# Three queries before a gate and five after, rows of w_o dealt by hand, and loops on VectorE and ScalarE

## The chip, the core and the metric

The kernel runs on one core of a Trainium2 chip. The metric is the time of one execution on the device in microseconds (us); where several executions are given, their median counts. A profiled execution also has a span, from its first to its last instruction, and all times inside the text are counted from the span's start.

A core has compute engines with a queue of instructions each: TensorE (PE in the profile; its weight loads are PEld), VectorE (DVE), ScalarE (ACT), GpSimd (POOL) and SyncE (SP), which here only issues transfers. Transfers between HBM and the on-chip memory SBUF are carried out by 16 DMA engines, and TensorE writes its sums to PSUM, here eight banks of 512 columns. Engines order themselves by semaphores: an instruction can add to one when it ends, and another can wait until one has reached a value.

## The reference, cut to what matters

One token is decoded: attention of 32 heads over a cache of 8192 keys and values each, with a gate from a small GLU beside it.

```python
xn = _layernorm(x, axis=-1)                      # x: 1 x 1 x 512
q = (xn @ wq).reshape(B, Sq, H, Dh)              # H = 32, Dh = 128
scores = einsum("bhqd,bhkd->bhqk", q, k_cache) * (Dh ** -0.5)
p = softmax(scores)
o = einsum("bhqk,bhkd->bhqd", p, v_cache)        # caches: 1 x 32 x 8192 x 128
s = o.reshape(B, Sq, H * Dh) @ wo                # wo: 4096 x 512
h = sigmoid(xn @ w_gate) * (xn @ w_up)           # 512 x 1376 each
g = silu(h @ w_down)                             # 1376 x 512
return x + s * g
```

All tensors are float32. The two caches are 134 MB each, out of 294 MB that the kernel reads.

## The kernel before

Two heads form a pair; there are 16 pairs (`NP`). A pair's keys are one load of 128 partitions by 16,384 columns (64 KB in each partition, 8.39 MB): 64 partitions for each head, 128 keys of 128 numbers in each. A pair's values have the same form. SBUF holds three slots of this size. K of even pairs goes into slot B, K of odd pairs into A, and V always into C; the last V goes into B, and w_o into C behind it. Before the pairs, A holds the three gate weights and C holds `wq`.

**One pair.** VectorE (`scores`, L295) multiplies the keys by the pair's query and sums over each key's 128 numbers, in two halves (L307, L309), then takes the largest score (L312). TensorE turns that column into a row (L339), VectorE reduces it (L314), TensorE spreads the result (L341), and ScalarE (`softmax`, L317) scales it, takes the exponentials (L323) and keeps their sums. TensorE then multiplies 32 times by V into the PSUM bank `po` (L350), ScalarE copies `po` out (L327), TensorE turns the parts together (L355), and ScalarE stores them in `heads` (L329). TensorE's work on the first 15 pairs is one loop (L385); on VectorE and ScalarE all 16 pairs are written out.

**The order of the loads** is that of SyncE's queue, and no planner changes it: `wq`, the gate, up and down weights, K0 in two halves, then K1 (L360), which waits for the gate because it overwrites the gate's weights, then V0 (L373), which waits for all eight queries because it overwrites `wq`. After that V and K alternate: V of pair n waits until TensorE has done with V of pair n-1 (`s_po`), and K of pair n+2 waits until VectorE has done with K of pair n (`k_free`, L375). K15 and V15 come in two halves. Last comes w_o (L382) in five pieces of 16, 8, 5, 2 and 1 rows in each partition (`WO`), a row having 2 KB, each piece with a semaphore of its own.

**The start.** `queries` (L234) makes the queries on TensorE, four heads at a time, eight times, into PSUM banks 0 to 7 by their number (L237); ScalarE copies each out in two halves (L245). The first four stand before the gate, the other four behind it (L250, L285). Between them VectorE weights the gate's and then the up matrix (`weighted`, L222 and L225), TensorE sums each over the partitions, column by column (L258, L259, into banks 4 and 5), ScalarE takes the sigmoid (L263), VectorE forms `hid` (L266) and weights the down matrix (L269 to L272), and TensorE sums it into `g_ps` (L279), bank 3. ScalarE takes its sigmoid into `g_row` (L283), and VectorE multiplies `g_row` by `g_ps` (L367) after the scores of pair 0. `busy` (L332) runs idle multiplications into `g_ps` near the end.

**The end.** When all heads are there, VectorE divides by the sums and turns the result (L395 to L404, `o_all`), and TensorE multiplies it by w_o, piece by piece as each lands: 24 rows into one bank (L414), which ScalarE copies (L423), then the rest and the copy into another (L418, L427). VectorE multiplies by `g_row` and adds x (L431, L433), and SyncE stores the 2 KB of output (L435).

Of the kernel before, what the change touches and what calls it, by code (L numbers as in the profile page):

```python
# [25 lines left out]
def kernel(  # L26
# [60 lines left out]
    mx = put("mx", 8)  # L87
# [13 lines left out]
    xnb = o1.rearrange("p (k m) -> p k m", m=P)  # L101
# [4 lines left out]
    wq_t = C.rearrange("p (k c) -> p k c", k=KT)  # L106
    wo_t = C.rearrange("p (r e) -> p r e", e=D)

    psum = nc.alloc_psum_tensor("psum", [P, 8 * QT], F32).ap()
    bank = [psum[:, i * QT:(i + 1) * QT] for i in range(8)]  # L110
    po, pt, pm, g_ps, acc, fold_ps, o_ps, oTl = bank


    sems = []
# [1 line left out]
    def semaphore(name):  # L116
        sems.append(nc.alloc_semaphore(name))
        return sems[-1]

    names = "x xr wg wu wd wr wq ka k0 k1 kb va vb".split()  # L120
    d = {n: Count(semaphore(f"d_{n}")) for n in names}
    WO = ((0, 16), (16, 24), (24, 29), (29, 31), (31, 32))
    d_wo = [Count(semaphore(f"d_wo{i}")) for i in range(len(WO))]
    d_v = semaphore("d_v")
# [11 lines left out]
    k_src = k_cache[0].rearrange("h (p j) e -> (h p) (j e)", p=HALF)  # L136
    v_src = v_cache[0].rearrange("h (p j) e -> (h p) (j e)", p=HALF)
    k_slot = lambda n: (B, A)[n % 2]
    k_sem = lambda n: d[f"k{n % 2}"]
    k_free = {}  # L140

    def rows_of(src, n):
        return src[n * P:(n + 1) * P, :]


    xv = x.rearrange("a b d -> (a b d)")
# [5 lines left out]
    d["wg"].by(sp.dma_start(wg_t, w_gate.rearrange("(p k) f -> p k f", k=KT)), 16)  # L152
    d["wu"].by(sp.dma_start(wu_t, w_up.rearrange("(p k) f -> p k f", k=KT)), 16)
    d["wd"].by(sp.dma_start(wd_t, w_down[:FP * P, :].rearrange("(p r) e -> p r e", r=FP)), 16)
    for name, c in (("ka", slice(0, SLOT // 2)), ("k0", slice(SLOT // 2, SLOT))):
        d[name].by(sp.dma_start(B[:, c], rows_of(k_src, 0)[:, c]), 16)


    s_pool.by(pool.memset(ident, 0.0))
# [14 lines left out]
    d["wr"].by(act.dma_start(wd_rest[:FL, :], w_down[FP * P:, :]), 16)  # L174
    dve.memset(st[:, 6:7], EPS)
    dve.memset(rs2, 0.0)
    for b in (4, 5):
        dve.memset(bank[b][:, :FP + 1], 0.0)
    dve.wait_ge(s_pool.sem, 2)
    for g in range(NG):  # L180
# [3 lines left out]
    def self_wait():  # L184
        dve.wait_ge(s_dve.sem, s_dve.n)
# [42 lines left out]
    n_xnb = s_dve.by(dve.tensor_copy(xnb, xn.rearrange("p (k o) -> p k o", o=1).to_broadcast([P, KT, P])))  # L228


    nq = H // NG
    n_qc = []

    def queries(lo, hi):  # L234
        with nc.Fori(lo, hi, engines=[pe.engine]) as t:
            for k in range(KT):
                m = pe.matmul(psum[:, bass.ds(t * QT, QT)], xnb[:, k, :], wq_t[:, k, bass.ds(t * QT, QT)],  # L237
                              start=(k == 0), stop=(k == KT - 1))
            m.then_inc(s_q, 1)
        for t in range(lo, hi):  # L240
            act.wait_ge(s_q, t + 1)
            pairs = slice(t * NG // 2, (t + 1) * NG // 2)
            for a in range(2):
                r = slice(a * HALF, (a + 1) * HALF)
                c = act.copy(q_all[r, pairs, :], bank[t][r, :].rearrange("p (n a d) -> p n a d", a=2, d=Dh)[:, :, a, :])  # L245
            n_qc.append(s_act.by(c))

    pe.wait_ge(d["wq"].sem, 16)
    pe.wait_ge(s_dve.sem, n_xnb)
    queries(0, nq // 2)  # L250

    turned = [bank[nq // 2 + a][:, :FP + 1] for a in range(2)]
    for a, (name, t) in enumerate((("wg", wg_t), ("wu", wu_t))):
        dve.wait_ge(d[name].sem, 16)
        weighted(t[:, 0, :], lambda k: t[:, k, :], lambda k: xn[:, k:k + 1], KT)
# [17 lines left out]
                                             op0=ALU.mult, op1=ALU.add))  # L273
    pool.wait_ge(s_dve.sem, n_wr)
    n_prz = s_pool.by(pool.memset(prz.rearrange("p j a -> p (j a)"), 0.0))
    pe.wait_ge(s_act.sem, n_qc[-1])
    pe.wait_ge(s_dve.sem, n_wr)
    for g in range(NG):
        m = pe.matmul(g_ps[g * GP:g * GP + 1, :GC], ones[:, 0:1], wd_t[:, 0, g * GC:(g + 1) * GC],  # L279
# [2 lines left out]
    act.wait_ge(s_pe.sem, n_gate)  # L282
    n_gs = s_act.by(act.activation(g_row, g_ps[:, :GC], AF.Sigmoid))  # L283
    act.wait_ge(s_pool.sem, n_prz)
    queries(nq // 2, nq)  # L285


    def load_k(n, parts=1):
        w = SLOT // parts
        for i in range(parts):  # L290
            c = k_sem(n) if i == parts - 1 else d["kb"]
            c.by(sp.dma_start(k_slot(n)[:, i * w:(i + 1) * w], rows_of(k_src, n)[:, i * w:(i + 1) * w]), 16)


    def scores(n):  # L295
        kt = k_slot(n).rearrange("p (j d) -> p j d", d=Dh)
        s = sc[n % 2]
        h = NB // 2
        q = q_all[:, n:n + 1, :].to_broadcast([P, h, Dh])
        first = {0: d["ka"], NP - 1: d["kb"]}.get(n)  # L300
        if first:
            dve.wait_ge(first.sem, 16)
        for i in range(2):
            if i == bool(first):
                dve.wait_ge(k_sem(n).sem, 16 * (n // 2 + 1))
            part = kt[:, i * h:(i + 1) * h, :]
            s_dve.by(dve.tensor_mul(part, part, q))  # L307
            self_wait()
            s_dve.by(dve.reduce_sum(s[:, i * h:(i + 1) * h], part, axis=AX.X))  # L309
        k_free[n] = s_dve.n  # L310
        self_wait()
        dve.reduce_max(mx[:, 0:1], s, axis=AX.X).then_inc(s_rm, 1)  # L312
        dve.wait_ge(s_pt, n + 1)
        dve.reduce_max(mx[:1, 2:4], pt[:1, :P].rearrange("p (a m) -> p a m", a=2), axis=AX.X).then_inc(s_am, 1)  # L314


    def softmax(n):  # L317
        act.wait_ge(s_pm, n + 1)
        s_act.by(act.mul(mx[:, 4:6], pm[:, 0:2], -SCALE))  # L319
        act.wait_ge(s_act.sem, s_act.n)  # L320
        for a in range(2):
            r = slice(a * HALF, (a + 1) * HALF)
            e = act.activation(prz[r, :, a], sc[n % 2][r, :], AF.Exp, bias=mx[r, 4 + a:5 + a], scale=SCALE,  # L323
                               accum_out=rs2[r, a:a + 1])
        e.then_inc(s_pr, 1)
        act.wait_ge(s_po, n + 1)
        act.copy(o1, po).then_inc(s_o1, 1)  # L327
        act.wait_ge(s_ot, n + 1)
        s_act.by(act.copy(heads[:, n, :], oTl[:, 0:4]))  # L329


    def busy(count):  # L332
# [37 lines left out]
    for n in range(NP - 1):  # L370
        if n:
            sp.wait_ge(s_po, n)
        sp.dma_start(C, rows_of(v_src, n)).then_inc(d_v, 16)  # L373
# [33 lines left out]
    pe.wait_ge(s_dve.sem, n)  # L407
    FOLD = WO[1][1]
    for (r0, r1), c in zip(WO, d_wo):
        pe.wait_ge(c.sem, 16)  # L410
        for r in range(r0, r1):
            if r < FOLD:
                g = r % NG
                m = pe.matmul(fold_ps[g * GP:g * GP + 1, :], o_all[:, r:r + 1], wo_t[:, r, :],  # L414
                              start=(r < NG), stop=(r >= FOLD - NG))
            else:
                for g in range(NG):
                    m = pe.matmul(acc[g * GP:g * GP + 1, :GC], o_all[:, r:r + 1],  # L418
                                  wo_t[:, r, g * GC:(g + 1) * GC], start=(r == FOLD), stop=(r == RW - 1))
# [49 lines left out]
```

## Time and profile before

| | |
|---|---|
| three runs | 687.00, 687.47 and 690.81 us; median 687.47 |
| the profiled execution | 687.28 us, of which the span has 685.4 |
| read from HBM | 293.67 MB |
| busy in the span | VectorE 588.5 us, TensorE 245.0 (weight loads 92.5), ScalarE 41.5, GpSimd 1.7 |

The page of the profile gives busy time by engine, then the span in 40 slices (a digit is the busy share in tenths; PEclk is the clock granted to TensorE), the DMA queues, the chain of work that ended last, and groups of equal instructions with their line, their number, busy time and mean, and the idle time before them with what ended it. In windows, the columns after the engines' busy time are the granted clock, the DMA share (1.00 is all 16 engines) and GB/s; a transfer's bytes and time count whole in the window where it starts, so that a short window can exceed 1. In the timeline a row is start, duration, engine, line, operation, and the number of instructions merged.

### The profile page before, as it was taken

Reading aid. Unit: us, or ns where it says so; the run is one execution under the profiler, and the core shown is the slowest. Engines: PE = TensorE matmul, PEld = TensorE weight load, DVE = VectorE, ACT = ScalarE, POOL = GpSimd, SP = SyncE. Lnnn points to the kernel's source line nnn. Section 1 sums busy time; section 2 is a strip of 40 time slices with the busy share of each in tenths; the row PEclk is TensorE's granted clock in tenths of the full one; section 3 lists DMA queues with packets and bytes.
Section 4 is the critical chain, followed back from the end, with each engine's and each line's share of the span. In section 5 each row is a group of like instructions: output and inputs, shape, how many; then the busy total and the mean of one; then the engine's idle time right before and its main releaser. Section 6 shows DMA issues by size and latency. Waiting matters only on the chain. (4 is left out here: it accounts for less than half of the span.)

```text
span 685.4 us, 3572 instructions
## 1 busy us (share of the span) xinstructions
PE 245.0 (36%) x1502; PEld 92.5 (14%) x1502; DVE 588.5 (86%) x145; ACT 41.5 (6%) x135; POOL 1.7 (0%) x10
## 2 busy tenths in 40 slices
PE   1595315050412405050422406060422406050486
PEld 0272101010110101010110101010110101010132
DVE  2259999999999999898989899898989899899930
ACT  0010110000000000000010100000010100000010
POOL 0000000000000000000000000000000000000000
PEclk9976856575665657575565757565665756565699
DMA  8999999999999999999999999999999999999996
GB/s 370 419 439 429 437 451 440 432 432 432 433 428 432 428 428 444 444 436 436 432 436 428 432 428 428 436 448 440 428 440 432 432 428 432 428 423 449 425 433 292
DMA packets 6501, 293.74 MB, mean 429 GB/s; under 512 B 760, under 2 KB 768, under 8 KB 1120
## 3 DMA queue, kind: packets, MB, share of 16 engines
q1 hardware_dynamic: 6344, 293.48, 99.1%
q10 hardware_dynamic: 152, 0.20, 0.1%
q8 instruction: 3, 0.05, 0.0%
q14 instruction: 2, 0.02, 0.0%
HBM read 293.67 MB, written 0.00 MB: 428 GB/s over the span
## 5 line engine op out<-in xcount | busy, mean ns | idle before, releaser
L307 DVE TENSOR_TENSOR slot<-slot,q_all 128x8192 f32<-128x8192 f32 x32 | 277.8, 8682 | 21.6 <-DMA slot<-in_A_k_cache_dram 21.6
L309 DVE TENSOR_REDUCE sc<-slot 128x64 f32<-128x8192 f32 x32 | 278.0, 8686 | 1.1
L350 PE MATMUL psum<-slot,prz 128*8 128x512 f32 x1024 | 143.9, 725 | 241.6 <-PEq L134 241.6
L350 PEld LDWEIGHTS psum<-slot,prz 128*8 128x8 f32 x1024 | 29.9, 102 | 342.0 <-issue 341.4
L339 PE MATMUL psum<-ident,mx 128*1 128x128 f32 x32 | 9.2, 387 | 119.4 <-PEq L134 119.4
L237 PE MATMUL psum<-slot,o 128*128 x64 | 32.1, 666 | 9.8 <-DMA slot<-in_A_wq_dram 9.8
L327 ACT COPY o<-psum 128x512 f32<-128x512 f32 x16 | 9.4, 586 | 397.6 <-PE psum L350 397.6
L355 PE MATMUL psum<-pick,o 128*128 128x2 f32 x128 | 16.4, 250 | 12.8 <-PEq L134 12.8
L355 PEld LDWEIGHTS psum<-pick,o 128*128 128x128 f32 x128 | 15.5, 191 | 27.2 <-issue 27.2
L339 PEld LDWEIGHTS psum<-ident,mx 128*1 128x1 f32 x32 | 1.8, 80 | 121.8 <-issue 121.8
L237 PEld LDWEIGHTS psum<-slot,o 128*128 128x128 f32 x64 | 13.6, 217 | 27.1 <-issue 27.1
L344 PE MATMUL psum<-rs,ones 128*128 128x2 f32 x32 | 8.7, 342 | 22.3 <-PEq L134 22.3
L222 DVE TENSOR_SCALAR slot<-slot,xn 128x1376 f32<-128x1376 f32 x2 | 1.9, 936 | 15.5 <-DMA slot<-in_B_w_gate_dram 15.0
L314 DVE TENSOR_REDUCE mx<-psum 1x2 f32<-1x128 f32 x16 | 4.4, 278 | 12.1 <-PE psum L339 12.1
L323 ACT ACTIVATE prz<-sc,mx 64x128 f32<-64x128 f32 x32 | 13.0, 406 | 0.7
L431 DVE TENSOR_TENSOR sc<-g_row,psum 128x128 f32<-128x128 f32 x1 | 0.3, 290 | 13.1 <-PE psum L418 13.1
L319 ACT ACTIVATE mx<-psum 128x2 f32<-128x2 f32 x16 | 2.8, 173 | 143.2 <-PE psum L341 143.2
L341 PE MATMUL psum<-mx,ones 1*128 1x2 f32 x32 | 8.6, 336 | 7.4 <-PEq L134 7.4
L344 PEld LDWEIGHTS psum<-rs,ones 128*128 128x128 f32 x32 | 7.8, 305 | 23.9 <-issue 23.9
L225 DVE SCALAR_TENSOR_TENSOR slot<-slot,xn 128x1376 f32<-128x1376 f32 x6 | 9.9, 1652 | 0.2
L395 DVE RECIPROCAL heads<-heads 128x32 f32<-128x32 f32 x1 | 0.4, 355 | 11.1 <-ACT heads L329 11.1
L341 PEld LDWEIGHTS psum<-mx,ones 1*128 1x128 f32 x32 | 7.7, 297 | 14.7 <-issue 14.7
(67 smaller groups left out, 84.0 us busy)
## 6 DMA issues: line engine op xcount, KB each, us to landing
slot<-in_A_k_cache_dram SPq DMA_DIRECT2D x4, 4096.0 KB, 45.5
slot<-in_A_v_cache_dram SPq DMA_DIRECT2D x2, 4096.0 KB, 37.5
slot<-in_A_wo_dram SPq DMA_DIRECT2D x1, 4096.0 KB, 20.7
slot<-in_B_w_gate_dram SPq DMA_DIRECT2D x1, 2752.0 KB, 28.2
slot<-in_B_w_up_dram SPq DMA_DIRECT2D x1, 2752.0 KB, 34.3
slot<-in_B_w_down_dram SPq DMA_DIRECT2D x1, 2560.0 KB, 39.8
slot<-in_A_wo_dram SPq DMA_DIRECT2D x1, 2048.0 KB, 25.2
slot<-in_A_wo_dram SPq DMA_DIRECT2D x1, 1280.0 KB, 27.7
```

The lines of the kernel that those rows point to most:

```text
L225: s_dve.by(dve.scalar_tensor_tensor(acc, t(k), col(k), acc, op0=ALU.mult, op1=ALU.add))
L237: m = pe.matmul(psum[:, bass.ds(t * QT, QT)], xnb[:, k, :], wq_t[:, k, bass.ds(t * QT, QT)], start=(k == 0), stop=(k == KT - 1))
L307: s_dve.by(dve.tensor_mul(part, part, q))
L309: s_dve.by(dve.reduce_sum(s[:, i * h:(i + 1) * h], part, axis=AX.X))
L314: dve.reduce_max(mx[:1, 2:4], pt[:1, :P].rearrange("p (a m) -> p a m", a=2), axis=AX.X).then_inc(s_am, 1)
L323: e = act.activation(prz[r, :, a], sc[n % 2][r, :], AF.Exp, bias=mx[r, 4 + a:5 + a], scale=SCALE, accum_out=rs2[r, a:a + 1])
L327: act.copy(o1, po).then_inc(s_o1, 1)
L339: pe.matmul(pt[:1, :P], mx[:, 0:1], ident, start=True, stop=True).then_inc(s_pt, 1)
L341: pe.matmul(pm[:, 0:2], ones[:1, :], mx[:1, 2:4], start=True, stop=True).then_inc(s_pm, 1)
L344: pe.matmul(oTl[:, 2:4], ones, rs2, start=True, stop=True)
L350: m = pe.matmul(po[g * GP:g * GP + 2 * ROWS, :], prz[:, j * ROWS:(j + 1) * ROWS, :], v[:, j * QT:(j + 1) * QT], start=(j < NG), stop=(j >= ...
L355: m = pe.matmul(oTl[:, 0:2], o1[:, b * Dh:(b + 1) * Dh], pick[:, 2 * b:2 * b + 2], start=(b == 0), stop=(b == ROWS - 1))
```

## The change

- **Queries.** Three stand before the gate instead of four, and five behind it. The first three use banks 0 to 2; the five use banks 1 to 5. The columns of gate and up move from banks 4 and 5 to 6 and 7, and `g_ps` becomes `po` (bank 0), while `busy` writes to bank 3, now called `idle`. TensorE's wait for ScalarE's copies ahead of the gate goes. Because `po` is overwritten by pair 0, VectorE multiplies `g_row` before the scores of pair 0.
- **Loops.** VectorE runs `scores` in a loop over two pairs, eight times; ScalarE runs `softmax` for pair 0, a loop over two pairs seven times, and pair 15 apart. The query's place in `q_all` and the place in `heads` come from a register. Semaphores that were counted up (`s_dve`, `k_free`, `s_pt`, `s_pm`, `s_po`, `s_ot`) are now waited for and taken down again by the waiting engine, in an instruction of its own (`take`), and `s_kf` and `s_vf` tell SyncE how many K and V slots have come free; `s_vf` is raised by ScalarE instead of TensorE. Each half of K has a semaphore; where K comes whole, SyncE raises the second itself after issuing the load.
- **w_o.** Of the first piece's 16 rows in each partition, 12 are loaded as before. The last four (8 KB in each partition) are loaded for partitions 0 to 79 in one transfer, and for partitions 80 to 127 in four transfers of 12 partitions. All six raise the first piece's semaphore.

```diff
-    po, pt, pm, g_ps, acc, fold_ps, o_ps, oTl = bank
+    po, pt, pm, idle, acc, fold_ps, o_ps, oTl = bank
+    g_ps = po
...
+    def load_k(n, parts=1):
+        w = SLOT // parts
+        for i in range(parts):
+            d[f"{'kh'[i]}{n % 2}"].by(sp.dma_start(k_slot(n)[:, i * w:(i + 1) * w], rows_of(k_src, n)[:, i * w:(i + 1) * w]), 16)
+        if parts == 1:
+            sp.sem_inc(d[f"h{n % 2}"].sem, 16)
...
-    for b in (4, 5):
+    for b in (6, 7):
         dve.memset(bank[b][:, :FP + 1], 0.0)
...
-    nq = H // NG
+    nq, n0 = H // NG, 3
...
-    queries(0, nq // 2)
-
-    turned = [bank[nq // 2 + a][:, :FP + 1] for a in range(2)]
+    queries(0, n0, 0)
+
+    turned = [bank[6 + a][:, :FP + 1] for a in range(2)]
...
-    pe.wait_ge(s_act.sem, n_qc[-1])
     pe.wait_ge(s_dve.sem, n_wr)
...
-    queries(nq // 2, nq)
+    queries(n0, nq, 1)
...
+    def tell_and_take(engine, sem, other):
+        engine.wait_ge(sem, 1).then_inc(other, 1)
+        take(engine, sem)
...
+        q = q_all[:, bass.ds(n, 1), :].to_broadcast([P, h, Dh])
         for i in range(2):
-            if i == bool(first):
-                dve.wait_ge(k_sem(n).sem, 16 * (n // 2 + 1))
+            take(dve, d[f"{'kh'[i]}{odd}"].sem, 16)
             part = kt[:, i * h:(i + 1) * h, :]
-            s_dve.by(dve.tensor_mul(part, part, q))
-            self_wait()
-            s_dve.by(dve.reduce_sum(s[:, i * h:(i + 1) * h], part, axis=AX.X))
-        k_free[n] = s_dve.n
-        self_wait()
+            dve.tensor_mul(part, part, q).then_inc(s_own, 1)
+            take(dve, s_own, i + 1)
+            dve.reduce_sum(s[:, i * h:(i + 1) * h], part, axis=AX.X).then_inc(s_own, 1)
+        tell_and_take(dve, s_own, s_kf)
         dve.reduce_max(mx[:, 0:1], s, axis=AX.X).then_inc(s_rm, 1)
-        dve.wait_ge(s_pt, n + 1)
+        take(dve, s_pt)
...
-        act.wait_ge(s_po, n + 1)
+        tell_and_take(act, s_po, s_vf)
         act.copy(o1, po).then_inc(s_o1, 1)
...
-    for n in range(NP):
-        if n % (NG // 2) == 0:
-            dve.wait_ge(s_act.sem, n_qc[n // (NG // 2)])
-        scores(n)
-        if n == 0:
-            dve.wait_ge(s_act.sem, n_gs)
-            s_dve.by(dve.tensor_mul(g_row, g_row, g_ps[:, :GC]))
-        softmax(n)
+    dve.wait_ge(s_act.sem, n_gs)
+    s_dve.by(dve.tensor_mul(g_row, g_row, g_ps[:, :GC]))
+    with nc.Fori(0, NP // 2, engines=[dve.engine]) as t:
+        for a in range(2):
+            dve.wait_ge(s_act.sem, n_qc[-a])
+            scores(t * 2 + a, a)
+    softmax(0, 0)
+    with nc.Fori(0, NP // 2 - 1, engines=[act.engine]) as t:
+        for a in range(2):
+            softmax(t * 2 + a + 1, 1 - a)
+    s_act.by(softmax(NP - 1, 1))
...
-            sp.wait_ge(s_po, n)
+            sp.wait_ge(s_vf, n)
...
-            sp.wait_ge(s_dve.sem, k_free[n])
+            sp.wait_ge(s_kf, n + 1)
...
     for (r0, r1), c in zip(WO, d_wo):
-        c.by(sp.dma_start(wo_t[:, r0:r1, :], wo.rearrange("(p r) e -> p r e", r=RW)[:, r0:r1, :]), 16)
+        few = FEW if r0 == 0 else 0
+        load_wo(c, r0, r1 - few)
+        if few:
+            load_wo(c, r1 - few, r1, 0, P - 4 * 12)
+            for p in range(P - 4 * 12, P, 12):
+                load_wo(c, r1 - few, r1, p, p + 12)
```

On VectorE, where the gate ends and the pairs begin, there stood (`slot_56` is B, `slot_55` is A, `sc_61` and `sc_62` are the two score tiles; x3 and the like are equal instructions in a row):

```order
L272 SCALAR_TENSOR_TENSOR slot_55<-wd_rest,hid,slot_55 96x512
L307 TENSOR_TENSOR slot_56<-slot_56,q_all 128x8192
L309 TENSOR_REDUCE sc_61<-slot_56 128x64
L307 TENSOR_TENSOR slot_56<-slot_56,q_all 128x8192
L309 TENSOR_REDUCE sc_61<-slot_56 128x64
L312 TENSOR_REDUCE mx<-sc_61 128x1
L314 TENSOR_REDUCE mx<-psum 1x2
L367 TENSOR_TENSOR g_row<-g_row,psum 128x128
```

and there stands now, with the line numbers of the changed kernel (`ISA` computes the query's place):

```order
L280 SCALAR_TENSOR_TENSOR slot_55<-wd_rest,hid,slot_55 96x512
L362 TENSOR_TENSOR g_row<-g_row,psum 128x128
L363 UNCONDITIONAL_BRANCH
L308 ISA
L308 TENSOR_TENSOR slot_56<-slot_56,q_all 128x8192
L310 TENSOR_REDUCE sc_61<-slot_56 128x64
L308 TENSOR_TENSOR slot_56<-slot_56,q_all 128x8192
L310 TENSOR_REDUCE sc_61<-slot_56 128x64
L312 TENSOR_REDUCE mx<-sc_61 128x1
L314 TENSOR_REDUCE mx<-psum 1x2
```

The multiplication of `g_row` has moved from behind the scores of pair 0 to ahead of them, and the scores stand in a loop; the semaphore instructions of `take` are not among these rows.

On SyncE, the end of the queue of loads was (`slot_57` is C):

```order
L379 DMA slot_56<-in_A_v_cache_dram 128x8192 x2
L382 DMA slot_57<-in_A_wo_dram 128x8192
L382 DMA slot_57<-in_A_wo_dram 128x4096
L382 DMA slot_57<-in_A_wo_dram 128x2560
L382 DMA slot_57<-in_A_wo_dram 128x1024
L382 DMA slot_57<-in_A_wo_dram 128x512
```

and is now:

```order
L382 DMA slot_56<-in_A_v_cache_dram 128x8192 x2
L387 DMA slot_57<-in_A_wo_dram 128x6144
L387 DMA slot_57<-in_A_wo_dram 80x2048
L387 DMA slot_57<-in_A_wo_dram 12x2048 x4
L387 DMA slot_57<-in_A_wo_dram 128x4096
L387 DMA slot_57<-in_A_wo_dram 128x2560
L387 DMA slot_57<-in_A_wo_dram 128x1024
L387 DMA slot_57<-in_A_wo_dram 128x512
```

The first piece of w_o has become six loads; the other four stand as before.

On ScalarE, the copies of the queries stand on both sides of the gate's two sigmoids, two to a query. Before:

```order
L245 COPY q_all<-psum 64x256 x8
L263 ACT_TABLE_LOAD
L263 ACTIVATE sg<-psum 128x11
L283 ACTIVATE g_row<-psum 128x128
L245 COPY q_all<-psum 64x256 x8
```

and now:

```order
L253 COPY q_all<-psum 64x256 x6
L271 ACT_TABLE_LOAD
L271 ACTIVATE sg<-psum 128x11
L290 ACTIVATE g_row<-psum 128x128
L253 COPY q_all<-psum 64x256 x10
```

Two copies, those of one query, have moved behind the gate, as that query's multiplications have on TensorE.

More of the change, by code (lines that the diff above doesn't have):

```diff
@@ L118, in semaphore @@
         return sems[-1]
-    names = "x xr wg wu wd wr wq ka k0 k1 kb va vb".split()
+    names = "x xr wg wu wd wr wq k0 k1 h0 h1 va vb".split()
     d = {n: Count(semaphore(f"d_{n}")) for n in names}
+    FEW = 4
     WO = ((0, 16), (16, 24), (24, 29), (29, 31), (31, 32))
@@ L128 @@
     s_pt, s_pm, s_po, s_ot = (semaphore(n) for n in ("s_pt", "s_pm", "s_po", "s_ot"))
+    s_own, s_kf, s_aown, s_vf = (semaphore(n) for n in ("s_own", "s_kf", "s_aown", "s_vf"))
     held = list(sems)
@@ L138 @@
     k_slot = lambda n: (B, A)[n % 2]
-    k_sem = lambda n: d[f"k{n % 2}"]
-    k_free = {}
     def rows_of(src, n):
         return src[n * P:(n + 1) * P, :]
+    def load_k(n, parts=1):
[4 more added lines that the diff above has]
+            sp.sem_inc(d[f"h{n % 2}"].sem, 16)
     xv = x.rearrange("a b d -> (a b d)")
@@ L154 @@
     d["wd"].by(sp.dma_start(wd_t, w_down[:FP * P, :].rearrange("(p r) e -> p r e", r=FP)), 16)
-    for name, c in (("ka", slice(0, SLOT // 2)), ("k0", slice(SLOT // 2, SLOT))):
-        d[name].by(sp.dma_start(B[:, c], rows_of(k_src, 0)[:, c]), 16)
+    load_k(0, 2)
     s_pool.by(pool.memset(ident, 0.0))
@@ L228, with queries @@
     n_xnb = s_dve.by(dve.tensor_copy(xnb, xn.rearrange("p (k o) -> p k o", o=1).to_broadcast([P, KT, P])))
-    nq = H // NG
+    nq, n0 = H // NG, 3
     n_qc = []
-    def queries(lo, hi):
+    def queries(lo, hi, first):
         with nc.Fori(lo, hi, engines=[pe.engine]) as t:
             for k in range(KT):
-                m = pe.matmul(psum[:, bass.ds(t * QT, QT)], xnb[:, k, :], wq_t[:, k, bass.ds(t * QT, QT)],
-                              start=(k == 0), stop=(k == KT - 1))
+                m = pe.matmul(psum[:, bass.ds(t * QT - (lo - first) * QT, QT)], xnb[:, k, :],
+                              wq_t[:, k, bass.ds(t * QT, QT)], start=(k == 0), stop=(k == KT - 1))
             m.then_inc(s_q, 1)
@@ L244, in queries @@
                 r = slice(a * HALF, (a + 1) * HALF)
-                c = act.copy(q_all[r, pairs, :], bank[t][r, :].rearrange("p (n a d) -> p n a d", a=2, d=Dh)[:, :, a, :])
+                c = act.copy(q_all[r, pairs, :], bank[first + t - lo][r, :].rearrange("p (n a d) -> p n a d", a=2, d=Dh)[:, :, a, :])
             n_qc.append(s_act.by(c))
@@ L284 @@
     act.wait_ge(s_pool.sem, n_prz)
-    queries(nq // 2, nq)
[L288 to L297, printed above, removed]
+    queries(n0, nq, 1)
+    def tell_and_take(engine, sem, other):
+        engine.wait_ge(sem, 1).then_inc(other, 1)
+        take(engine, sem)
@@ L298, in scores @@
+    def scores(n, odd):
+        kt = k_slot(odd).rearrange("p (j d) -> p j d", d=Dh)
+        s = sc[odd]
         h = NB // 2
[L299 to L302, printed above, removed]
+        q = q_all[:, bass.ds(n, 1), :].to_broadcast([P, h, Dh])
         for i in range(2):
-            if i == bool(first):
-                dve.wait_ge(k_sem(n).sem, 16 * (n // 2 + 1))
+            take(dve, d[f"{'kh'[i]}{odd}"].sem, 16)
@@ L314, in scores, with softmax @@
         dve.reduce_max(mx[:1, 2:4], pt[:1, :P].rearrange("p (a m) -> p a m", a=2), axis=AX.X).then_inc(s_am, 1)
[L317 to L320, printed above, removed]
+    def softmax(n, odd):
+        take(act, s_pm)
+        act.mul(mx[:, 4:6], pm[:, 0:2], -SCALE).then_inc(s_aown, 1)
+        take(act, s_aown)
         for a in range(2):
             r = slice(a * HALF, (a + 1) * HALF)
-            e = act.activation(prz[r, :, a], sc[n % 2][r, :], AF.Exp, bias=mx[r, 4 + a:5 + a], scale=SCALE,
+            e = act.activation(prz[r, :, a], sc[odd][r, :], AF.Exp, bias=mx[r, 4 + a:5 + a], scale=SCALE,
@@ L324, in softmax @@
                                accum_out=rs2[r, a:a + 1])
         e.then_inc(s_pr, 1)
-        act.wait_ge(s_po, n + 1)
+        tell_and_take(act, s_po, s_vf)
         act.copy(o1, po).then_inc(s_o1, 1)
-        act.wait_ge(s_ot, n + 1)
-        s_act.by(act.copy(heads[:, n, :], oTl[:, 0:4]))
+        take(act, s_ot)
+        return act.copy(heads[:, bass.ds(n, 1), :], oTl[:, 0:4].rearrange("p (o c) -> p o c", o=1))
     def busy(count):
         for _ in range(count):
-            pe.matmul(g_ps, ones, q_all[:, :QT // Dh, :], start=True, stop=True)
+            pe.matmul(idle, ones, q_all[:, :QT // Dh, :], start=True, stop=True)
@@ L371, with load_wo @@
         if n:
-            sp.wait_ge(s_po, n)
+            sp.wait_ge(s_vf, n)
         sp.dma_start(C, rows_of(v_src, n)).then_inc(d_v, 16)
         if n + 2 < NP:
-            sp.wait_ge(s_dve.sem, k_free[n])
+            sp.wait_ge(s_kf, n + 1)
             load_k(n + 2, 2 if n + 2 == NP - 1 else 1)
-    sp.wait_ge(s_dve.sem, k_free[NP - 2])
+    sp.wait_ge(s_kf, NP - 1)
     for name, c in (("va", slice(0, SLOT // 2)), ("vb", slice(SLOT // 2, SLOT))):
         d[name].by(sp.dma_start(B[:, c], rows_of(v_src, NP - 1)[:, c]), 16)
-    sp.wait_ge(s_po, NP - 1)
+    sp.wait_ge(s_vf, NP - 1)
+    wo_src = wo.rearrange("(p r) e -> p r e", r=RW)
+    def load_wo(c, r0, r1, p0=0, p1=P):
+        c.by(sp.dma_start(wo_t[p0:p1, r0:r1, :], wo_src[p0:p1, r0:r1, :]), 16)
     for (r0, r1), c in zip(WO, d_wo):
-        c.by(sp.dma_start(wo_t[:, r0:r1, :], wo.rearrange("(p r) e -> p r e", r=RW)[:, r0:r1, :]), 16)
+        few = FEW if r0 == 0 else 0
[4 more added lines that the diff above has]
+                load_wo(c, r1 - few, r1, p, p + 12)
     pe.wait_ge(s_act.sem, n_qc[-1])
@@ L409 @@
     for (r0, r1), c in zip(WO, d_wo):
-        pe.wait_ge(c.sem, 16)
+        pe.wait_ge(c.sem, c.n)
         for r in range(r0, r1):
```

## The prediction

> **What bounds the kernel now.** I read the page first: the total, the DMA slices and the queues.
>
> ```profile
> span 685.4 us, 3572 instructions
> DMA  8999999999999999999999999999999999999996
> DMA packets 6501, 293.74 MB, mean 429 GB/s; under 512 B 760, under 2 KB 768, under 8 KB 1120
> q1 hardware_dynamic: 6344, 293.48, 99.1%
> q8 instruction: 3, 0.05, 0.0%
> q14 instruction: 2, 0.02, 0.0%
> ```
>
> All but the first and the last slice show 9, and q1, on which SyncE's loads run, fills 99.1% of what 16 DMA engines could do in the whole span. So the kernel is 293.74 MB through 16 busy DMA engines: 429 / 16 = 26.8 GB/s for each, or 0.306 us for 8 KB. A compute engine matters only where it lets a DMA engine run dry, or behind the last landing. The groups of instructions and the DMA issues say how far VectorE is from doing that.
>
> ```profile
> L307 DVE TENSOR_TENSOR slot<-slot,q_all 128x8192 f32<-128x8192 f32 x32 | 277.8, 8682 | 21.6 <-DMA slot<-in_A_k_cache_dram 21.6
> L414 PE MATMUL psum<-slot,o_all 128*1 128x512 f32 x48 | 7.0, 748 | 2.3 <-DMA slot<-in_A_wo_dram 2.3
> DMA to landing us min/median/max: 27.1/29.3/30.0
> slot<-in_A_k_cache_dram SPq DMA_DIRECT2D x14, 41.8
> ```
>
> VectorE waits for K 21.6 us in nine waits, 2.4 us each: it is quicker than the DMA. A load of 8.39 MB takes 8.39 / 0.429 = 19.6 us; V (the third row) lands 27.1 to 30.0 us after its issue and K after 41.8, so each load stands in the queue for 7.5 us or more before its turn. That is the cover for whatever delays an issue.
>
> The last landings are read from windows of half a microsecond and from the chain that ended last.
>
> ```profile
> 679.50:680.00 0.50, 0.41 (x4) 0.00 (x0) 0.00 (x0) 0.02 (x1) 0.00 (x0) 1.00 0.97 385
> 680.00:680.50 0.50, 0.00 (x0) 0.00 (x0) 0.00 (x0) 0.50 (x1) 0.00 (x0) 1.00 0.53 205
> 680.50:681.00 0.50, 0.32 (x12) 0.31 (x16) 0.00 (x0) 0.06 (x1) 0.00 (x0) 1.00 0.31 123
> 681.00:681.50 0.50, 0.50 (x28) 0.47 (x21) 0.00 (x0) 0.00 (x0) 0.00 (x0) 1.00 0.16 61
> 681.50:682.00 0.50, 0.50 (x29) 0.47 (x22) 0.00 (x0) 0.00 (x0) 0.00 (x0) 1.00 0.25 70
> 682.00:682.50 0.50, 0.50 (x25) 0.31 (x14) 0.00 (x0) 0.00 (x0) 0.00 (x0) 1.00 0.01 4
> q8 instruction: 1, 0.02, 4.8%
> ```
>
> The last two columns are the DMA share and GB/s. Until 680.0 all engines run; then 0.53, 0.31, 0.16 of them, and after 682.0 one row of 2 KB (4 GB/s for 0.5 us) is left. The 0.25 holds a fetch of code that comes after the loads (last row, of the window 681.5 to 683.1: 4.8% of 16 x 1.6 us = 1.23 us on one engine); without it about 0.1. So the engines end over 2 us, two or three of them late. Evened out they would end at 680.0 + 0.5 x (0.53 + 0.31 + 0.16 + 0.25 + 0.01) - 1.23 / 16 = 680.55, against about 682.15. **The most that evenness can bring is 1.6 us**, and nothing in this change cuts bytes.
>
> ```profile
> 2.00:2.50 0.50, 0.00 (x0) 0.00 (x0) 0.00 (x0) 0.00 (x0) 0.09 (x1) 1.00 4.70 1573
> 2.50:3.50 1.00, 0.00 (x0) 0.00 (x0) 0.71 (x8) 0.00 (x0) 0.70 (x4) 1.00 0.66 262
> 1.02 0.39 SPq L148 DMA_DIRECT2D slot<-in_A_wq_dram  x1
> ```
>
> The first load's rows are 65,536 bytes and count whole where they start: 1573 x 0.5 = 786 KB, 12 engines, start by 2.5, and 262 KB, four engines, only up to 1 us later. After that all run without a pause, so who starts late should end late.
>
> **Three and five queries.** The timeline around the gate:
>
> ```profile
> 38.08 5.03 DVE L225 SCALAR_TENSOR_TENSOR slot<-slot,xn 128x1376 f32<-128x1376 f32 x3
> 40.32 4.47 PE L258 MATMUL psum<-ones,slot 128*128 128x1 f32 x20
> 44.97 4.65 PE L258 MATMUL psum<-ones,slot 128*128 128x1 f32 x20
> 58.53 8.68 DVE L307 TENSOR_TENSOR slot<-slot,q_all 128x8192 f32<-128x8192 f32 x1
> 58.75 0.61 PE L279 MATMUL psum<-slot,ones 128*1 128x128 f32 x8 [8.81 <-DVE slot L272]
> 59.42 0.33 SPq L292 DMA_DIRECT2D slot<-in_A_k_cache_dram  x1
> 59.42 0.28 ACT L283 ACTIVATE g_row<-psum 128x128 f32<-128x128 f32 x1 [14.10 <-PE psum L279]
> 68.28 0.75 ACT L245 COPY q_all<-psum 64x256 f32<-64x256 f32 x2 [2.69 <-PE psum L237]
> 71.72 0.75 ACT L245 COPY q_all<-psum 64x256 f32<-64x256 f32 x2 [2.69 <-PE psum L237]
> 75.14 0.33 SPq L373 DMA_DIRECT2D slot<-in_A_v_cache_dram  x1
> ```
>
> A query costs TensorE 71.72 - 68.28 = 3.44 us. With one less, the gate columns start near 36.9 instead of 40.32; the up columns must then wait for VectorE (38.08 + 5.03 = 43.11) and start at 43.2 instead of 44.97. So `hid`, the gate and the issue of K1 come 1.75 us earlier: K1 at 57.7.
>
> ```profile
> 58.00:60.00 2.00, 1.25 (x9) 0.64 (x10) 2.00 (x2) 0.28 (x1) 0.31 (x1) 0.50 1.06 459
> 60.00:62.00 2.00, 2.00 (x3) 0.67 (x2) 2.00 (x1) 0.00 (x0) 0.00 (x0) 0.50 1.53 659
> 62.00:64.00 2.00, 2.00 (x5) 0.97 (x4) 2.00 (x1) 0.00 (x0) 0.00 (x0) 0.75 0.56 229
> ```
>
> From 58 to 64 the DMA share averages 1.05: there is no hole that an earlier K1 could fill, only a queue that it lengthens. Worth 0; the cover is K0's own transfer.
>
> V0 pays for it: its issue waits for all queries, and five stand behind the gate. 75.14 - 1.75 + 3.44, and 1.75 us more of them lie under the granted clock of 0.50 (it holds until about 63), which does half the work, +0.9: 77.7. V0 landed at 75.14 + 27.1 = 102.2, so its transfer began by 102.2 - 19.6 = 82.6 on the last engine and, by the 2 us over which engines end, from 80.6 on the first. The first load was issued at 1.02 and moved from 2.0 on twelve engines, by 3.5 on four. V0 issued at 77.7 is thus ready at 78.7 to 80.2: covered, by some 1 to 2 us instead of 4. Worth 0, and a rival below.
>
> VectorE's multiplication of `g_row` now stands before the loop and waits for TensorE and ScalarE: 59.42 + 0.28 + 0.3 = 60.0, less 1.75, is 58.3 against 58.53. Level. It could not stay behind the scores, since the gate's sum now lies in `po`.
>
> **The loops.** Per pair VectorE gets about seven semaphore instructions more. The traces show no price for one; the chain of waits has 0.04 us between engines as the nearest row, so I take 0.05 to 0.1 each, 0.35 to 0.7 per pair, with nothing and 1 us as ends. The 2.4 us wait per pair covers it. The last two pairs run without a wait, but behind them there is room:
>
> ```profile
> 652.39 0.04 issue
> 669.72 0.19 DVE L404 COPY o_all<-psum 128x32 f32<-128x32 f32 x1 [0.50 <-PE psum L401]
> 672.88 7.03 PE L414 MATMUL psum<-slot,o_all 128*1 128x512 f32 x48 [2.26 <-DMA slot<-in_A_wo_dram]
> ```
>
> `o_all` is done at 669.9 and TensorE waits for w_o until 672.88: 3 us, enough for two pairs at 1 us. V's issue now goes by ScalarE (`s_vf`) and K's by one more VectorE instruction: 0.1 us each against 7.5. SyncE's extra increments follow a DMA and delay none. Sum of the loops: 0. Shorter programs might drop fetches of code, which cost DMA time: a fetch on q8 (window 81 to 82.2) took 5.1% x 16 x 1.2 = 0.98 us of one engine and one on q14 (61 to 62.2) 0.31.
>
> ```profile
> q8 instruction: 1, 0.02, 5.1%
> q14 instruction: 1, 0.01, 1.6%
> ```
>
> Whose code it is the trace does not say: I count 0, with up to 0.98 at the low end.
>
> **The four rows of w_o.** Before, each engine takes 8 of 128 partitions; 8 KB of four rows each. Now 80 partitions give 5 to each of 16, and 4 x 12 partitions one each to twelve engines: 9 for twelve, 5 for four. Price: +0.31 us on twelve and -0.92 us on four. SyncE issues ten loads instead of five, some 4.5 us by its 0.43 each, while V15 still moves until about 671: hidden.
>
> [...]
>
> If the four that start late are the four relieved, the latest goes from 682.15 to 681.25, and the best of the others, ending near 680.9 (share 0.16 after 681.0 is two or three engines), rises to 681.2: even. **Gain 0.9 us at the last landing.** Behind it stands TensorE:
>
> ```profile
> 680.68 1.27 PE psum L418 x40
> ```
>
> L414 ended at 672.88 + 7.03 = 679.91, so L418 can start 0.75 us sooner without anything else moving. I take 0.8: span 684.6, and with the profiled run's 687.28 us **686.5 us**. That run is 0.2 below the median of 687.47 of the three.
>
> **Rivals.** (1) The deal misses, the change not doing what its name says: the late engines are among the twelve, and the end moves by +0.31, 687.6; or a load of 12 rows goes to four engines only, which then have 5 + 12 = 17 instead of 8 rows, +2.75: 690.0. For it: the rows show that four start late, not which, and a fetch of code delays whichever engine carries it. Chance 0.25. (2) Everything evens out, with fetches gone: -1.6, 685.7. Against it: twelve engines get more. 0.12. (3) Slower: V0 comes late. The DMA runs dry if the eighth query ends after about 79.5. The price is the clock's: had 0.50 held through all five queries, they would take 5 x 6.9 = 34 us from 57.6, V0 would move near 93 instead of 81, and the time be about 699; 7 us more of 0.50 would cost about 1.5, 688.8. Against it: the clock was back at 1.00 from 63 on. 0.08, mostly at the small price. (4) Slower: each jump back fetches code. VectorE has 7 and ScalarE 6 jumps back; 13 fetches at 0.31 to 0.98 us, all on one DMA engine of the sixteen that bound the kernel, give 4 to 13 us: 691 to 700. Against it: TensorE's loop over 15 pairs already jumps back 14 times, and the whole span has five fetches. 0.05. [...]
>
> **How the numbers follow.** The forecast has 0.50. The range starts at 685.4, rival 2 less the 0.3 by which the lowest run lies under the profiled one, and ends at 689.0, which takes in the first half of rival 1 and the small price of 3. A measurement of this kernel can tell about 0.5%, 3.4 us, from no change. Faster than that is out of reach of 1.6 us: 0.03 is for what I have not seen. Slower by more is rival 4 and the dear part of 3: 0.09. Same: 0.88.
>
> **What would show it.** Right: windows after 680 fall to nothing by 681.3 to 681.5; K1's issue at 57.7, V0's at 77 to 78 with no dip in the share near 81; about 2 us of K wait per pair left. Wrong: a share under 0.8 between 80 and 84, more than five instruction packets on q8 and q14, or `o_all` after w_o's first landing.

## The result and the profile after

The changed kernel takes 691.69 us in the median of 8 runs (691.13 to 699.02), beside 687.07 for the kernel before on the same chip (8 runs, 686.72 to 690.81). The ratio is 1.0073 (95% interval 1.0051 to 1.0096): 4.6 us slower, more than the 0.5% that can be told from no change, and outside the predicted range. The profiled execution took 691.25 us, 3.97 more than the one of before.

The page of the changed kernel, in the rows that were read of before:

```profile
span 689.4 us, 3856 instructions
DMA  8999999999999999999999999999999999999997
GB/s 368 416 436 453 442 426 441 426 426 430 430 449 441 437 430 426 430 426 449 437 437 437 426 430 426 437 449 434 441 426 426 430 430 449 420 432 456 413 372 255
DMA packets 6693, 293.74 MB, mean 426 GB/s; under 512 B 824, under 2 KB 832, under 8 KB 1184
q1 hardware_dynamic: 6536, 293.48, 99.2%
q8 instruction: 3, 0.05, 0.0%
q14 instruction: 2, 0.02, 0.0%
```

The same bytes, DMA engines as busy as before, and 4 us more. The DMA engines don't run dry; they are slower while they work. The row of GB/s says where: in the last slice but one the share still reads 9, but the rate is 372. So the place is looked for by GB/s and not by the share. In windows of 2 us (the last two columns are the DMA share and GB/s) the changed kernel has:

```profile
666.00:668.00 2.00, 2.00 (x24) 0.50 (x20) 0.00 (x0) 0.00 (x0) 0.00 (x0) 1.00 1.02 422
668.00:670.00 2.00, 1.66 (x16) 0.20 (x8) 0.00 (x0) 0.10 (x1) 0.00 (x0) 1.00 1.03 233
670.00:672.00 2.00, 1.38 (x9) 1.19 (x10) 0.04 (x1) 0.64 (x2) 0.00 (x0) 1.00 1.09 205
672.00:674.00 2.00, 1.77 (x6) 0.52 (x4) 0.91 (x4) 0.00 (x0) 0.00 (x0) 1.00 1.15 164
674.00:676.00 2.00, 0.19 (x1) 0.00 (x0) 0.00 (x0) 0.00 (x0) 0.00 (x0) 1.00 0.82 184
676.00:678.00 2.00, 0.90 (x8) 0.24 (x12) 0.00 (x0) 0.00 (x0) 0.00 (x0) 0.97 0.92 385
```

and the kernel before, at the same place:

```profile
666.00:668.00 2.00, 1.21 (x12) 0.89 (x9) 0.00 (x0) 0.59 (x1) 0.00 (x0) 1.00 1.06 459
668.00:670.00 2.00, 1.85 (x7) 0.82 (x7) 0.95 (x4) 0.16 (x1) 0.00 (x0) 1.00 0.87 377
670.00:672.00 2.00, 0.62 (x2) 0.00 (x0) 0.00 (x0) 0.00 (x0) 0.00 (x0) 1.00 0.94 401
672.00:674.00 2.00, 1.12 (x12) 0.34 (x16) 0.00 (x0) 0.00 (x0) 0.00 (x0) 1.00 0.97 418
674.00:676.00 2.00, 2.00 (x12) 0.34 (x8) 0.00 (x0) 0.00 (x0) 0.00 (x0) 0.50 0.99 422
676.00:678.00 2.00, 2.00 (x16) 0.44 (x12) 0.00 (x0) 0.00 (x0) 0.00 (x0) 0.65 0.98 416
```

For 8 us the engines show a share of 0.82 to 1.15 at half the rate or less. The six windows add up to 1593 GB/s, and to 2493 in the kernel before: 900 less, and 900 / 429 x 2 us = 4.2 us. (Against the mean of 429 in every window it would be 4.6.) The profiled execution is 4.0 us longer, so **the whole loss lies here**, where the dealt rows of w_o are moved. Through the last landing it comes to the end. The chain of the changed kernel:

```profile
655.30 29.27 DMA slot<-in_A_wo_dram
684.57 0.04 issue
684.62 1.27 PE psum L432 x40
```

The landing came at 680.64 before (680.68 less the 0.04 of issue), 3.9 us earlier; the steps behind it are the same.

### The profile page after: what moved, and what is told of

Same layout as the page of the kernel before. It is cut to its first block, busy times and chain, and to the rows that moved or that the text cites. A ratio compares the mean times of both kernels' runs of the same rounds, so it can differ in the third digit from the quotient of the medians.

```text
span 689.4 us, 3856 instructions
## 1 busy us (share of the span) xinstructions
PE 250.7 (36%) x1502; PEld 93.6 (14%) x1502; DVE 589.2 (85%) x145; ACT 41.5 (6%) x135; POOL 1.7 (0%) x10
## 3 DMA queue, kind: packets, MB, share of 16 engines
q1 hardware_dynamic: 6536, 293.48, 99.2%
## 5 line engine op out<-in xcount | busy, mean ns | idle before, releaser
L308 DVE TENSOR_TENSOR slot<-slot,q_all 128x8192 f32<-128x8192 f32 x32 | 278.0, 8686 | 13.8 <-DVEq L137 13.7
L350 PE MATMUL psum<-slot,prz 128*8 128x512 f32 x1024 | 148.1, 743 | 212.1 <-PEq L137 212.1
L409 DVE RECIPROCAL heads<-heads 128x32 f32<-128x32 f32 x1 | 0.4, 353 | 13.1 <-ACT heads L329 13.1
## 6 DMA issues: line engine op xcount, KB each, us to landing
slot<-in_A_v_cache_dram SPq DMA_DIRECT2D x2, 4096.0 KB, 37.1
```

What stands on the lines that cost most here:

```text
L308: dve.tensor_mul(part, part, q).then_inc(s_own, 1)
L350: m = pe.matmul(po[g * GP:g * GP + 2 * ROWS, :], prz[:, j * ROWS:(j + 1) * ROWS, :], v[:, j * QT:(j + 1) * QT], start=(j < NG), stop=(j >= ...
```

## The experiments

The trace also has one record for each DMA packet, with its start, bytes and duration; it names neither the DMA engine nor the partitions. For the 128 packets of 8 KB that carry the four dealt rows, these give the table below for every kernel that moves them (ns; "first" and "last" are the first and the last 64 by start).

```
kernel              loads of the four rows            mean  first  last
after               80 + 4 x 12 partitions             658    554    762
e2_deal_alone       the same, on the kernel before     651    529    774
e3_step_four        80 + 4 x 12, every fourth one      576    517    634
e4_split_128        128                                309    309    309
e5_near_source      80 + 4 x 12, another source        644    521    766
e6_two_halves       64 + 64                            618    579    658
e7_eights           16 x 8, partitions 0-63 first      443    309    578
e8_eighty_and_48    80 + 48                            587    529    646
e9_eights_turned    16 x 8, partitions 64-127 first    480    574    385
```

**The parts alone.** e1_plain_wo is the changed kernel without the deal; e2_deal_alone is the kernel before with the deal and nothing else.

```diff
-    FEW = 4
+    FEW = 0
```

> The changed kernel with w_o loaded as before (no dealing); loops and the three and five queries stay. Theory A (the dealt loads of w_o, whose 8 KB packets took 658 ns in the mean instead of 309, cost everything): all of it comes back, 686.8 to 687.6, and w_o's first landing is near 673. Theory B (loops and queries make a part of the 4.6 us, for example by a later o_all): 688.5 or more.

> The kernel before with the dealt w_o alone: no loops, four and four queries. Theory A: all of the loss is there, 691 to 692. Theory B: less than 690.

e1: 686.92 us, ratio to the kernel before 0.9999 (0.9989 to 1.0008). e2: 692.04, ratio 1.0077 (1.0060 to 1.0094). The deal alone is the whole loss; queries and loops together are worth nothing measurable. e2 has the same hole of rate:

```profile
668.00:670.00 2.00, 1.85 (x8) 0.91 (x8) 0.94 (x4) 0.16 (x1) 0.00 (x0) 1.00 1.07 242
670.00:672.00 2.00, 0.72 (x2) 0.00 (x0) 0.00 (x1) 0.00 (x0) 0.00 (x0) 1.00 1.00 168
```

**What in the deal.** In e3 the loads of 12 take every fourth partition instead of 12 neighbours; in e4 the four rows are still a load of their own, but one of 128 partitions.

```diff
...
-            for p in range(P - 4 * 12, P, 12):
-                load_wo(c, r1 - few, r1, p, p + 12)
+            for p in range(P - 4 * 12, P - 4 * 12 + 4):
+                load_wo(c, r1 - few, r1, p, P, 4)
```

(The last argument, which e7 and e9 use too, is the step from one partition to the next.)

```diff
-            load_wo(c, r1 - few, r1, 0, P - 4 * 12)
-            for p in range(P - 4 * 12, P, 12):
-                load_wo(c, r1 - few, r1, p, p + 12)
+            load_wo(c, r1 - few, r1)
```

> The changed kernel; the four loads of 12 partitions take every fourth of the partitions 80 to 127 instead of 12 neighbours. Same bytes, same loads, same number of rows for each DMA engine. Theory P (many engines write into few neighbouring partitions at once and hold each other up): the 8 KB packets of these four loads come down from about 700 towards 309 ns, and the time falls to 687 to 689.5. Theory S (the number of loads, or pieces of 8 KB, are slow by themselves): no change, 691 to 692.

> The changed kernel; the last four rows of the first piece of w_o come in one load over all 128 partitions, so that nothing is dealt but the pieces are of 24 KB and 8 KB as in the change. Theory P: 8 KB packets take about 309 ns, time 686.8 to 687.8. Theory S: packets of 8 KB are slow here too, 690 or more.

e3: 691.49 us, ratio 1.0069 (1.0052 to 1.0086); e4: 687.22, 1.0012 (0.9992 to 1.0032). e4's windows show the full rate:

```profile
670.00:672.00 2.00, 1.77 (x6) 0.76 (x7) 0.95 (x4) 0.16 (x1) 0.00 (x0) 0.98 1.09 463
672.00:674.00 2.00, 2.00 (x10) 0.16 (x12) 0.00 (x0) 0.00 (x0) 0.00 (x0) 0.50 1.01 434
```

So neither pieces of 8 KB nor a load more cost anything: all 128 packets take 309 ns. What costs must lie in how the loads cut up the 128 partitions. Spreading the 12 partitions hardly helped (576 ns for 658), so the theory in its first form, that the 12 neighbours get in each other's way, fell. It took a wider form, a supposition that e5 to e9 test: in a load of 128 partitions each engine writes to 8 partitions of its own; in any other these groups are dealt otherwise, and an engine then writes where another one is writing.

**Where the bytes come from.** In e5 the loads of 80 and 12 partitions stay, but read pieces of 8 KB that lie behind one another in HBM, as no other load of w_o does; the four rows then hold other rows of w_o.

```diff
+            flat = wo.rearrange("(q r) e -> q r e", r=few)
-            load_wo(c, r1 - few, r1, 0, P - 4 * 12)
-            for p in range(P - 4 * 12, P, 12):
-                load_wo(c, r1 - few, r1, p, p + 12)
+            for p0, p1 in [(0, P - 4 * 12)] + [(p, p + 12) for p in range(P - 4 * 12, P, 12)]:
+                c.by(sp.dma_start(wo_t[p0:p1, r1 - few:r1, :], flat[p0:p1, :, :]), 16)
```

> The changed kernel; the five dealt loads read their 8 KB pieces of w_o from one another's neighbourhood (8 KB apart, not 64 KB), so the four rows hold other rows of w_o. Destination, number and sizes stay. Theory P2 (the loss is on SBUF's side: a DMA engine is fast into partitions that are its own in a load of 128, and two engines that write into the same group of partitions share its rate): no change, 8 KB packets near 650 ns, 691 to 692. Theory H (the order of addresses in HBM): packets come down towards 309 ns, 687 to 689.

e5: 691.56 us, ratio 1.0062 (1.0046 to 1.0077), and the packets as slow as in the changed kernel (644 ns for 658). So the order of the source's addresses is not the cause.

**Which partitions.** e6 takes two loads of 64 partitions, e8 one of 80 and one of 48, and e7 sixteen loads of 8 partitions, each with one partition out of eight neighbouring fours, first in 0 to 63 and then in 64 to 127. All three have no load of 12.

```diff
-            load_wo(c, r1 - few, r1, 0, P - 4 * 12)
-            for p in range(P - 4 * 12, P, 12):
-                load_wo(c, r1 - few, r1, p, p + 12)
+            load_wo(c, r1 - few, r1, 0, HALF)
+            load_wo(c, r1 - few, r1, HALF, P)
```

```diff
...
-            load_wo(c, r1 - few, r1, 0, P - 4 * 12)
-            for p in range(P - 4 * 12, P, 12):
-                load_wo(c, r1 - few, r1, p, p + 12)
+            for p in range(0, P, 32):
+                for j in range(4):
+                    load_wo(c, r1 - few, r1, p + j, p + 32, 4)
```

```diff
             load_wo(c, r1 - few, r1, 0, P - 4 * 12)
-            for p in range(P - 4 * 12, P, 12):
-                load_wo(c, r1 - few, r1, p, p + 12)
+            load_wo(c, r1 - few, r1, P - 4 * 12, P)
```

> The changed kernel; the four rows come in two loads of 64 partitions, 0 to 63 and 64 to 127: each DMA engine has four rows in each, nothing is dealt. Theory P2 with groups that repeat within a half: two engines for each group, packets of 8 KB double to about 618 ns, 2.5 us more, 689 to 690. Theory K (only loads that do not use all 16 engines, or rows that 16 does not divide evenly, are slow): packets 309 ns, 687.

> The changed kernel; the four rows come in 16 loads of 8 partitions, each fourth of 32. Eight rows go to eight engines, so these have 16 rows of 8 KB and the others none: 2.5 us more for these in any case, 689.5. Theory P2: the loads of partitions 0 to 63 run at about 309 ns, as each engine writes into its own group, and those of 64 to 127 are slow, since the other eight engines write there meanwhile: packets up to 618 ns, 690 to 692. Theory K: all 128 packets alike.

> The changed kernel; the load of 80 partitions stays, the four of 12 become one of 48: 5 and 3 rows for each engine, nothing dealt, all 16 engines in each load. Theory P2: the load of 80 is as slow as in the change (two thirds of its packets above 450 ns), the load of 48 too: 689 to 691. Theory K in its form that only loads of 12 are slow: packets 309 ns, 687.

e6: 692.02 us, ratio 1.0059 (1.0043 to 1.0076); e7: 691.99, 1.0058 (1.0033 to 1.0084); e8: 691.25, 1.0052 (1.0034 to 1.0070). Loads of 12 are not needed for the loss. e6's packets took the 618 ns that were expected, but its time is 2 to 3 us above what was expected of it: that sum had no price for the other pieces in the queue, whose packets slowed down too (16 KB up to 2031 ns). e7 tells most, for its packets are of two kinds: the first 64, which by the order of the queue go to partitions 0 to 63, take 309 ns, and the last 64, to 64 to 127, take 578 in the mean. The windows change with them:

```profile
668.00:670.00 2.00, 1.04 (x13) 1.02 (x10) 0.00 (x0) 0.58 (x1) 0.00 (x0) 1.00 1.06 447
670.00:672.00 2.00, 1.77 (x7) 0.69 (x6) 0.95 (x4) 0.16 (x1) 0.00 (x0) 1.00 1.07 287
672.00:674.00 2.00, 0.57 (x2) 0.00 (x0) 0.00 (x0) 0.00 (x0) 0.00 (x0) 1.00 1.15 238
674.00:676.00 2.00, 0.00 (x0) 0.00 (x0) 0.00 (x0) 0.00 (x0) 0.00 (x0) 1.00 0.93 213
```

Up to 670 the rate is full; then it halves. At 670, and again from 672 to 674, the records have eight packets of 8 KB under way at a time and eight of 16 KB beside them: eight engines carry the small loads, and the other eight have gone on to the next piece, a load of 128 partitions. While the small loads go to 0 to 63, neither is slowed: from 668 to 670, 8 KB take 309 ns and 16 KB 611. From 672 to 674, with 64 to 127 in turn, they take 622 and 1250 in the mean. Both double, as they would if the other eight write to 64 to 127 and the two sets meet there. That e7 is no faster than the others although half of its packets are has a plain reason beside this: eight engines carry all 128 rows, 8 more than in e4 for each, or 8 x 0.309 = 2.5 us.

**The order turned.** If that is so, the same loads with 64 to 127 first must be slow first and fast afterwards. If merely the later loads of a long row are slow, they stay slow last.

```diff
-            for p in range(0, P, 32):
+            for p in (64, 96, 0, 32):
```

> The 16 loads of 8 partitions again, those of partitions 64 to 127 first and those of 0 to 63 last. Theory P2: slow and fast change places: the first 64 packets of 8 KB near 615 ns while the other eight engines write into the same partitions, the last 64 near 309; DMA at about half its rate first, then full. Theory Q (many small loads in the queue slow what comes late): fast first, slow last, as before.

A single execution: 691.54 us beside 686.78 before. The first 64 packets take 574 ns in the mean and the last 64 take 385: the first 22 of these still lie above 400, and from about 674.5 on they take 309. From 669.5 to 672 the 16 KB packets beside them take 1248 ns in the mean, and 612 from 674.8 to 677. The slow kind has changed places, as the windows show:

```profile
668.00:670.00 2.00, 2.00 (x24) 0.50 (x20) 0.00 (x0) 0.00 (x0) 0.00 (x0) 1.00 1.04 246
670.00:672.00 2.00, 1.03 (x11) 0.25 (x3) 0.00 (x0) 0.59 (x1) 0.00 (x0) 1.00 1.04 217
672.00:674.00 2.00, 1.77 (x11) 0.94 (x10) 0.76 (x3) 0.16 (x1) 0.00 (x0) 1.00 0.97 234
674.00:676.00 2.00, 1.35 (x4) 0.52 (x4) 0.19 (x1) 0.00 (x0) 0.00 (x0) 1.00 0.91 374
676.00:678.00 2.00, 0.77 (x4) 0.14 (x8) 0.00 (x0) 0.00 (x0) 0.00 (x0) 0.71 1.04 442
```

Why the change to fast comes some 2 us after the 64th packet, while e7's change to slow comes nearly at once, the records don't show. No run moves such a load with the other engines idle; that the slowing needs them rests on both kinds of packets doubling together, and being fast together.

**The loops alone.** e10 is e1 with four queries ahead of the gate again, so that only the loops are left of the change.

```diff
-    FEW = 4
+    FEW = 0
...
-    nq, n0 = H // NG, 3
+    nq, n0 = H // NG, 4
...
-    queries(n0, nq, 1)
+    queries(n0, nq, 2)
```

> The changed kernel with w_o loaded as before, four queries ahead of the gate (banks 0 to 3) and four behind it (banks 2 to 5): the loops alone. If loops and queries are each worth nothing: 686.5 to 687.5, K1 issued near 59.5, V0 near 75.5. If the two cancelled in the run with plain w_o: off by more than 0.7 us either way.

e10: 687.16 us, ratio 0.9996 (0.9964 to 1.0027). Beside e1's 0.9999, this says that three and five queries are worth nothing measurable either, though e10's interval alone would leave room for 2 us. The issues of K1 and V0 in e10, and then in e1:

```profile
60.00 0.33 SPq L150 DMA_DIRECT2D slot<-in_A_k_cache_dram  x1
76.01 0.33 SPq L376 DMA_DIRECT2D slot<-in_A_v_cache_dram  x1
```

```profile
57.40 0.33 SPq L150 DMA_DIRECT2D slot<-in_A_k_cache_dram  x1
76.88 0.33 SPq L376 DMA_DIRECT2D slot<-in_A_v_cache_dram  x1
```

## Why the prediction was wrong, point by point

**The bound was right.** The kernel is its bytes through 16 busy DMA engines (q1 at 99.1% before and 99.2% now), the place of the loss is the DMA, and what lies beside it (e1: 0.9999) cost nothing.

**Three and five queries: right.** Between e10 and e1, K1's issue moves 2.6 us ahead and V0's 0.9 us back. In the changed kernel they stand at 57.9 and 78.1, where 57.7 and 77.7 were forecast, and no dip in the share follows V0's issue. That the two issues came so close is in part luck: e1 has the same code up to w_o, and 57.4 and 76.9. The rows of the changed kernel:

```profile
57.90 0.33 SPq L150 DMA_DIRECT2D slot<-in_A_k_cache_dram  x1
78.06 0.33 SPq L376 DMA_DIRECT2D slot<-in_A_v_cache_dram  x1
58.65 8.69 DVE L308 TENSOR_TENSOR slot<-slot,q_all 128x8192 f32<-128x8192 f32 x1
```

```profile
78.00:80.00 2.00, 0.03 (x1) 0.00 (x0) 2.00 (x1) 0.73 (x2) 0.00 (x0) 1.00 1.21 524
80.00:82.00 2.00, 0.00 (x0) 0.00 (x0) 2.00 (x1) 0.00 (x0) 0.00 (x0) 0.64 1.28 524
82.00:84.00 2.00, 0.00 (x0) 0.00 (x0) 2.00 (x1) 0.00 (x0) 0.00 (x0) 0.50 0.94 401
```

Rival 3, a late V0, did not come. `g_row` ahead of the scores was level, as forecast: the first multiplication starts at 58.65 instead of 58.53.

**The loops: right in their worth, a little low in their price.** The same half of the keys, pair by pair, in the kernel before and then in the changed one:

```profile
130.75 8.67 DVE L307 TENSOR_TENSOR slot<-slot,q_all 128x8192 f32<-128x8192 f32 x1
166.76 8.67 DVE L307 TENSOR_TENSOR slot<-slot,q_all 128x8192 f32<-128x8192 f32 x1
202.76 8.67 DVE L307 TENSOR_TENSOR slot<-slot,q_all 128x8192 f32<-128x8192 f32 x1
```

```profile
132.45 8.69 DVE L308 TENSOR_TENSOR slot<-slot,q_all 128x8192 f32<-128x8192 f32 x1 [0.49 <-DVEq L137]
169.11 8.69 DVE L308 TENSOR_TENSOR slot<-slot,q_all 128x8192 f32<-128x8192 f32 x1
206.20 8.69 DVE L308 TENSOR_TENSOR slot<-slot,q_all 128x8192 f32<-128x8192 f32 x1 [0.43 <-DVEq L137]
```

A pair took 36.0 us and takes 36.7 and 37.1 in turn: 0.9 us more in the mean, where 0.35 to 0.7 was taken and 1 was the upper end. Each second pair, behind a jump back, has an idle 0.4 to 0.5 us of its own. The wait for K covers it through the pairs: VectorE's idle time before this line is 13.7 us in ten pieces, the longest 2.0, where it was 21.6. At the end the cover is nearly used up, as e1 shows, where w_o is not late:

```profile
671.45 0.19 DVE L418 COPY o_all<-psum 128x32 f32<-128x32 f32 x1 [0.50 <-PE psum L415]
672.44 3.61 PE L428 MATMUL psum<-slot,o_all 128*1 128x512 f32 x32
```

`o_all` is done at 671.64, 1.7 us later than before, and TensorE starts on w_o at 672.44: 0.8 us are left of the 3. Rival 4 was wrong: the loops jump back 13 times and the page has five instruction packets (three on q8, two on q14), as before, so no jump added a fetch of code. Why none did, and on which engine fetches fall, no run shows. Nor did a shorter program drop a fetch.

**The four rows of w_o: this is where it failed.** The step was "Price: +0.31 us on twelve and -0.92 us on four". It counted the rows for each engine and gave a row the time that it takes in a load of 128 partitions. The count held: packets under 512 B went from 760 to 824, and the 64 more are of 4 bytes, as many as 16 for the load of 80 partitions and 12 for each load of 12 (before, q1 has 708 of them, 16 for each of 44 loads of 128 partitions and 4 for the store); and with the packets followed from the end of one to the start of the next, nine of 8 KB on twelve engines and five on four fit the records. The +0.31 and -0.92 us no run shows, because the time of a row did not stay: 309 ns in e4, 658 in the mean in the changed kernel, so the 128 rows alone take 128 x (658 - 309) / 16 = 2.8 us more of every engine. The neighbours in the queue pay as well. By the packet records, the 128 packets of 16 KB behind them took up to 2191 ns instead of 611, all together 1.5 us more of every engine, and the 24 KB ones ahead of them up to 1948 instead of 912, 0.2 us more. That sums to 4.5 us, beside 4.0 by which the profiled execution was longer, and 4.6 in the medians. In place of -0.8 stood +4.6.

None of the rivals held it. Rival 1 let the deal miss the late engines or pile rows on four, which again is a count at a fixed price, and ends at 690.0. What the experiments showed in its place: a row's time depends on the partitions that it is written to (309 ns in 0 to 63 and 622 in 64 to 127, both in e7) and, it is inferred, on who else writes there. e4 against the others shows that neither the size of the pieces nor a further load decides; e7 and e9 show that the same loads are fast or slow by the half of the partitions they go to, and that the other engines' packets are slowed in the same stretch. That the other engines write to 64 to 127 in that stretch is inferred, since no record names partitions. How the partitions are grouped, and why the 12 neighbours of a load are slow, no run shows either. The forecast asked how many engines a load of 12 uses, and not which partitions these then write to.

**Could another deal have brought the 0.9 us?** Where both are slow in e7, 8192 bytes take 0.622 us and 16,384 take 1.250: 13.2 + 13.1 = 26.3 GB/s together, and a single engine has 429 / 16 = 26.8. If that is what a group of partitions takes, an engine from elsewhere adds nothing to it, and rows taken from a late engine can be written no sooner by another. This is argued from these numbers; none of the nine versions that deal or split the rows was faster than before. Whether the deal made the engines end more evenly stays open: what they lost on the way hides it.

## What to carry to other kernels

Price a load that does not span the 128 partitions as the others do by who writes where, and not by rows for each engine alone: in e7 the packets took twice their time (622 ns for 309) where, by the account above, two engines met, and the other engine's took twice theirs (1250 for 611). A share of busy DMA engines near 1 doesn't show this (in the changed kernel it was 1.15 from 672 to 674, at 164 GB/s); read GB/s beside it, and the duration of single packets of one size. Before work is shifted from one engine to another, ask whether the time of a piece stays the same there.

## What the runs showed of the hardware

- Beside full-width loads, loads of 8 partitions ran at full rate on partitions 0 to 63 (e7: 309 ns for 8 KB) and at half of it on 64 to 127 (622 ns), and the other engines' packets with them: 16 KB rose from 611 ns to 1250 in e7, and to as much as 2191 in the changed kernel.
- With another source in HBM the slowing stays (644 ns, e5), and with a load of 128 partitions it is gone (309 ns, e4).
- Loads of 64 partitions in e6 were no better than one of 80 and one of 48 in e8: 618 and 587 ns, though 64 rows divide evenly among 16 engines.
- Loops over two pairs with their semaphores cost VectorE 0.9 us for each pair of 36, and no additional fetch of code (five instruction packets, as before).
